# A new order for the first 560 steps of an attention and MLP kernel, without five of its eight identity products

## The chip, the cores and the metric

The kernel runs on one core of one Trainium2 chip. The metric is device time in microseconds (us). The kernel before takes 633.52 us, the median of three runs (633.43 to 633.88). The profile used below is one further execution of it.

## The reference

```python
def _attn_ref(q, k, v):                       # (4, 8, 768, 64) each
    k_sum = k.reshape(B, H, nb, 32, D).max(axis=3)
    v_sum = v.reshape(B, H, nb, 32, D).mean(axis=3)
    scores_l = scale * np.matmul(q, k.transpose(0, 1, 3, 2))
    mask_l = np.abs(pos[:, None] - pos[None, :]) < 16
    scores_s = scale * np.einsum('bhsd,bhnd->bhsn', q, k_sum) + np.log(32)
    scores_all = np.concatenate([np.where(mask_l, scores_l, -1e9), scores_s], axis=-1)
    a = softmax(scores_all)
    return np.matmul(a, np.concatenate([v, v_sum], axis=2))
def _moe_ref(x, w_in, w_out):                 # x (3072, 512), d_ff 2048
    h = x @ w_in
    return ((h * np.cos(h)) @ w_out).astype(np.float32)
```

Each query sees the keys nearer than 16 positions and 24 block summaries. The attention output, heads side by side, is the x of the MLP.

## The kernel before, in words

The 3072 tokens are eight blocks of 384 (0 to 7). Two blocks make one batch entry. In a block the eight heads are four pairs, called a, b, c, d: `a0` is the first pair of block 0. The MLP of a block runs over 16 slices of d_ff; slice `w5` is 128 columns of w_in and 128 rows of w_out. One slice applied to one block is a step, `s0` to `s127`; s0 to s5 are block 0 with slices 0 to 5, s6 to s21 are block 1, s22 to s31 the rest of block 0.

Nothing is scheduled by the compiler. The string `ORDER` lists some 2,100 tokens. Each token calls one method, and the tokens' order is the order in which each engine's queue receives its instructions. An engine takes its own in that order and waits at the first that is not ready. The semaphores between engines follow from which tile or PSUM bank an instruction reads and writes. A token has a name, a step and arguments: numbers are PSUM banks or buffers, and a letter at the end is the engine (a = ScalarE, v = VectorE, p = GpSimd). All loads and stores sit in SyncE's queue, but for the very last store.

The tokens that matter here, in the order in which a pair goes through them, for blocks 0 and 1:

- `q`, `k` load the pair (L454); `tq`, `tk` transpose it on TensorE (L503, L516); `cq`, `ck` copy the result out of PSUM (L509 or L511, L370 or L372), and `ks` takes the block maxima of k (L535, VectorE).
- `ms` puts the masks into two PSUM banks (L554), `sc` adds the scores (L579), `mx` takes the row maxima (L597, VectorE, two instructions), `ex` the exponentials (L614, ScalarE, six instructions), `iv` the inverse of the sums (L624 and L627), `nm` multiplies by it (L630, GpSimd).
- `tp` transposes the probabilities (L639), `cp` copies them out (L370 or L372), `v` loads the value windows (L475, L483), `m` copies the value summaries beside them, `va` is the product with the values (L683). `xh` and `xl` split the result into two parts, the MLP's input (L370 or L372, L376).
- The means of v come from `vm` and `ve` for batch entry 0, and for entry 1 from loads `v1_0.l`, `v1_1.l`, ... (L246), each followed by its sum `v1_0.s`, ... (L261 on VectorE, L251 and L270 on GpSimd). These loads share one buffer: `v1_1.l` waits until `v1_0.s` is done, `v1_2.l` until `v1_1.s` is done.
- A weight slice is loaded by `l` (L391, L395) as packed bytes, and unpacked by `ab` and `sh` (ScalarE, L403, L409), `fb` (VectorE, L416), `hi` (L370 or L372) and `lo` (L376).
- A step is `u` in four chunks, one for each pair's x, or `up` in one piece (L738, L726); `tu`, `re`, `si`, `ga` are the gate (L746, L749, L754, L758); `hi` and `lo` split it; `dh` and `dl` are the products with w_out (L786).

The eight `h` tokens are products of the identity with itself (L930, 128x512) whose result nothing reads:

```python
        def products(self, i):
            nc.tensor.matmul(
                out=bank(i), lhsT=ident, rhs=ident.unsqueeze(1).broadcast_to([P, DM // P, P]), start=True, stop=True
            )
```

Three of them (h0, h2, h4) come before the first transposes, five (h7, h5, h1, h6, h3) between the attention's products of the first 30 us.

Of the kernel before, what the change touches and what calls it, by code (L numbers as in the profile page):

```python
# [47 lines left out]
s5.lo.1.v w9.hi.a w6.l.6 s6.tu.1 s10.up.6 w8.lo.p a2.v a2.m s3.re s6.re s5.dh s3.si s3.ga s3.hi.1.v w7.ab.1 w9.lo.v
s4.dl s3.lo.0.p s4.dh s3.dh v1_5.s.v w7.sh w10.ab.0 s3.dl s5.dl w7.fb w7.hi.v s6.si s6.ga s8.up.2 s6.hi.0.v w10.sh
s11.tu.0 s6.lo.0.v w10.fb s5.ta.0.a s10.tu.1 w10.hi.a w10.lo.p w7.lo.v s9.up.4 s11.re s10.re s5.ta.1.v s11.si s10.si  # L50
w6.ab.1 s7.up.1 s11.ga v1_6.l s10.ga w12.l.7 v1_6.s.v s10.hi.1.a w6.sh s10.lo.1.v v1_7.l s6.dh.5.7.6 w6.fb w12.ab.0
s11.hi.0.a s6.dl s11.lo.0.v w6.hi.a s5.ta.2.v s7.tu.1 s8.tu.0 s7.re s10.dh s11.dh s10.dl v1_7.s.v s11.dl w12.sh s7.si
s8.re w13.l.6 s7.ga s16.up.0 s8.si s8.ga s8.hi.1.a s15.up.1 w12.fb s7.hi.0.a s14.up.2 a2.k s5.st.0 w6.lo.v w12.hi.a
w13.ab.1 s7.lo.1.p s7.dh a2.kt.1 s15.tu.1 s5.st.1 s15.re w13.sh s5.st.2 s8.lo.0.p w12.lo.v s15.si s15.ga w15.l.7
a2.kt.0 b2.k s8.dl s8.dh w13.fb w11.l.6 s14.tu.0 s15.hi.0.a s14.re s14.si s7.dl s15.lo.0.v s16.tu.1 s15.dh s15.dl
s16.re s14.ga s14.hi.1.v s14.lo.1.p s12.up.3 w13.hi.a a2.ks.1 s16.si s16.ga a2.q s16.hi.0.a s16.lo.0.v s12.tu.0
b2.kt.0 w15.ab.0 s13.up.1 w13.lo.v w15.sh s18.up.0 s19.up.2 b2.kt.1 s13.tu.1 a2.ks.0 c2.k w15.fb b2.ks.0 w11.ab.1
w11.sh b2.ks.1 s12.re s16.dl s14.dh s12.si s13.re w11.fb s16.dh s12.ga w15.hi.a a2.qt s12.hi.1.a s14.dl w11.hi.v
s13.si s12.lo.0.v c2.kt.0 s13.ga s18.tu.0 s13.hi.0.a w14.l.6 w11.lo.p s18.re s18.si s18.ga s12.dh s18.hi.1.v s12.dl
s13.lo.1.v s19.tu.1 c2.kt.1 s18.lo.0.p s19.re d2.k s9.tu.0 s13.dh s9.re w14.ab.1 s19.si w15.lo.p s9.si w14.sh s18.dh  # L60
s18.dl s13.dl s19.ga s9.ga w14.fb s19.hi.0.a w14.hi.a a2.kw.v s9.hi.1.v s17.up.0 s23.up.3 b2.q a2.sc.2.1 w14.lo.p
b2.kw.a s19.lo.0.v d2.kt.1 d2.kt.0 a2.z.1 s19.dh a2.z.0 s19.dl a2.mx.2 s17.tu.1 s17.re s17.si s9.dh b2.qt s17.ga c2.q
# [974 lines left out]
```

## Time and profile before

| | |
|---|---|
| median of three runs | 633.52 us |
| profiled execution, its own time | 633.6 us |
| its span, first to last instruction | 631.9 us |
| TensorE busy | 621.1 us, 98% |
| VectorE, ScalarE, GpSimd busy | 422.1, 323.9, 204.6 us |

The span is what the profile shows; 1.7 us of the execution's own time lie outside it. Matmul ends are modelled: a TensorE instruction may look busy until the next one starts. In a timeline row the first number is the start and the second the time from there to the end of the row's last instruction.

### The profile page before, as it was taken

To read this page: it belongs to the slowest core of one execution; us is meant where nothing else is said; L and a number is where in the kernel's file an instruction comes from. 1 tells how busy PE (TensorE), PEld (TensorE's weight loads), DVE (VectorE), ACT (ScalarE), POOL (GpSimd) and SP (SyncE) were. 2 spreads that over 40 slices of the span, in tenths; PEclk is the share of its full clock that TensorE was granted. 3 is DMA by queue.
4 is the path that set the end of the run, shared out by engine and by line. 5 is a ranking of instruction groups with operands and counts; after the bars stand their busy time and mean duration, and the time that the engine had idled before them with its cause. 6 is when DMAs were issued, how large, how long until landed. Compare 5 with 4: busy or idle time off the path is not lost.

```text
span 631.9 us, 12130 instructions
## 1 busy us (share of the span) xinstructions
PE 621.1 (98%) x4568; PEld 544.3 (86%) x4568; DVE 422.1 (67%) x814; ACT 323.9 (51%) x606; POOL 204.6 (32%) x218
## 2 busy tenths in 40 slices
PE   8989999999999999999999999999999999999997
...
PEclk9999999999999999999999999999999999999999
...
GB/s 223 261 220 272 297 123 250 145 54 123 122 143 133 112 95 174 102 61 108 109 110 126 117 93 102 121 47 77 108 98 61 117 75 56 114 35 17 1 1 50
DMA packets 170058, 73.52 MB, mean 116 GB/s; under 512 B 136848, under 2 KB 158864, under 8 KB 170000
## 3 DMA queue, kind: packets, MB, share of 16 engines
...
q14 instruction: 22, 0.18, 0.1%
...
## 4 chain that ended last, share of the span: by engine, by line
PE 92%; DVE 4%; SPq 2%; DMA 1%; issue 1%; ACT 1%; POOL 0%; POOLq 0%; DVEq 0%
PE banks L786 41%; PE banks L726 40%; PE banks L683 3%; PE banks L567 3%; PE banks L930 1%; SPq L475 1%; DVE stage L416 1%; PE banks L738 1%; PE banks L579 1%; SPq L483 1%; PE banks L516 0%; PE banks L909 0%; DMA late<-in_v_dram 0%; DMA x<-in_v_dram 0%; DVE kd L535 0%
## 5 line engine op out<-in xcount | busy, mean ns | idle before, releaser
L726 PE MATMUL banks<-xh,w 128*128 128x384 f32 x976 | 255.5, 337 | 0.5 <-DVE t L758 0.5
L786 PE MATMUL banks<-w,gh 128*128 128x512 f32 x768 | 196.5, 392 | 0.1
L726 PEld LDWEIGHTS banks<-xh,w 128*128 128x128 f32 x976 | 176.8, 188 | 3.1 <-issue 0.8
L786 PEld LDWEIGHTS banks<-w,gh 128*128 128x128 f32 x768 | 142.6, 188 | 31.4 <-DVE gh L372 1.8
L726 PE MATMUL banks<-xl,w 128*128 128x384 f32 x488 | 163.2, 334 | 0.0
L376 POOL TENSOR_TENSOR gl<-t,gh 128x384 fp32r<-128x384 f32 x63 | 65.9, 1048 | 283.3 <-DVE gh L372 147.8
L746 ACT ACTIVATE t<-banks 128x384 int32<-128x384 f32 x128 | 62.0, 488 | 126.8 <-PE banks L726 59.7
L749 DVE SCALAR_TENSOR_TENSOR t<-t,banks 128x384 f32<-128x384 int32 x128 | 69.1, 546 | 68.3 <-ACT t L746 67.6
L786 PE MATMUL banks<-w,gl 128*128 128x512 f32 x384 | 108.0, 392 | 0.0
L754 ACT ACTIVATE t<-t 128x384 f32<-128x384 f32 x128 | 65.9, 523 | 63.4 <-DVE t L749 63.1
L726 PEld LDWEIGHTS banks<-xl,w 128*128 128x128 f32 x488 | 91.6, 188 | 0.4
L758 DVE TENSOR_TENSOR t<-t,banks 128x384 f32<-128x384 f32 x128 | 69.4, 547 | 33.1 <-ACT t L754 32.1
L786 PEld LDWEIGHTS banks<-w,gl 128*128 128x128 f32 x384 | 71.6, 188 | 15.7 <-POOL gl L376 0.5
L370 ACT CAST gh<-t 128x384 fp32r<-128x384 f32 x66 | 33.5, 511 | 43.5 <-DVE t L758 25.5
L630 POOL TENSOR_TENSOR sc<-sc,r 128x720 f32<-128x720 f32 x28 | 39.0, 1392 | 43.5 <-DVE r L627 41.0
L602 POOL TENSOR_TENSOR sc<-sc,m 128x720 f32<-128x720 f32 x24 | 34.3, 1433 | 49.6 <-DVE m L594 49.6
L376 DVE TENSOR_TENSOR gl<-t,gh 128x384 fp32r<-128x384 f32 x65 | 36.8, 569 | 12.5 <-ACT gh L370 7.5
L372 DVE CAST gh<-t 128x384 fp32r<-128x384 f32 x62 | 23.1, 373 | 18.1 <-PE banks L786 14.9
L586 DVE SCALAR_TENSOR_TENSOR sc<-banks,mask 128x360 f32<-128x360 f32 x48 | 24.5, 523 | 12.5 <-PE banks L567 12.2
L620 DVE TENSOR_REDUCE r<-sc 128x6 f32<-128x726 f32 x24 | 21.6, 902 | 13.8 <-ACT sc L609 13.8
L376 POOL TENSOR_TENSOR w<-stage,w 128x1024 fp32r<-128x1024 f32 x8 | 19.8, 2470 | 31.3 <-DVE w L372 20.0
L609 ACT ACTIVATE sc<-sc 128x720 f32<-128x720 f32 x24 | 19.4, 807 | 19.0 <-POOL sc L602 18.8
...
## 6 DMA issues: line engine op xcount, KB each, us to landing
...
```

The lines of the kernel that those rows point to most:

```text
L370: eng.copy(out=out, in_=in_)
L372: eng.tensor_copy(out=out, in_=in_)
L376: eng.tensor_tensor(out=lo, in0=src, in1=hi.bitcast(F32), op=ALU.subtract)
L586: nc.vector.scalar_tensor_tensor(out=self.sc.rearrange("p (c h) n -> p c h n", h=2)[:, :, hh, :], in0=self.sp[hh], scalar=SCALE, in1=mask[ ...
L602: nc.gpsimd.tensor_tensor(out=self.sc, in0=self.sc, in1=self.m.unsqueeze(2).broadcast_to([P, U, NK]), op=ALU.subtract)
L630: nc.gpsimd.tensor_tensor(out=self.sc, in0=self.sc, in1=self.r.unsqueeze(2).broadcast_to([P, U, NK]), op=ALU.mult)
L726: nc.tensor.matmul(out=self.h, lhsT=w_of(name, self.f)[:, c * P : (c + 1) * P], rhs=x_of(self.blk, part, c), start=n == 0, stop=n == last,)
L746: nc.scalar.activation(out=self.t.bitcast(I32), in_=self.h, func=AF.Copy, scale=1.0 / TWO_PI, bias=0.25)
L749: nc.vector.scalar_tensor_tensor(out=self.t, in0=self.t.bitcast(I32), scalar=-TWO_PI, in1=self.h, op0=ALU.mult, op1=ALU.add)
L754: nc.scalar.activation(out=self.t, in_=self.t, func=AF.Sin, scale=-1.0, bias=-0.5 * math.pi)
L758: nc.vector.tensor_tensor(out=self.t, in0=self.t, in1=self.h, op=ALU.mult)
L786: nc.tensor.matmul(out=accs[self.run][i], lhsT=g[:, i * P : (i + 1) * P], rhs=w_of(name, self.f), start=self.first and n == 0, stop=self.l ...
```

## The change

`ORDER` alone is changed. It has 2,093 tokens instead of 2,098: h7, h5, h1, h6 and h3 are gone, h0, h2 and h4 stay. Every other token is there once, as before. SyncE's queue (loads and stores) keeps its order exactly. On TensorE, VectorE, ScalarE and GpSimd the order is new up to `c2.z.0` in block 2, and from there to the end the two strings are the same but for line breaks. In the new part 58 tokens change between VectorE, ScalarE and GpSimd, and many take other PSUM banks. Cut to the part up to the first product with w_out:

```diff
-h0.w.3 h2.w.0 h4.w.1 a0.k a0.q b0.q a0.tk.1.5 c0.k a0.tk.0.0 a0.ms.7.6 a0.ks.1 d0.k b0.tq.3 a0.ks.0 b0.k a0.tq.4 c0.q
-a0.ck.1.a a0.ck.0.a h7.w.5 b0.cq.a a0.cq.v a0.sc c0.tk.0.0 c0.tk.1.2 b0.tk.0.4 c0.ks.0 c0.ck.0.a a0.mx.0 w1.l.6 h5.w.1
-a1.q c0.tq.0 h1.w.1 d0.q a0.ex.0 c0.ck.1.v b0.ck.0.a d0.tk.0.6 c0.ks.1 a0.iv b0.tk.1.1 b0.ks.0 d0.tk.1.2 c0.ms.3.7
-c0.cq.v b0.ms.5.0 c0.sc v0_0.l d0.ck.1.a d0.ks.1 b0.ck.1.a d0.ks.0 b0.ks.1 d0.ck.0.v b0.sc w1.ab.0 b1.q w1.sh c0.mx.1
-h6.w.2 a1.tq.6 a1.ms.1.4 v0_1.l v1_0.l d0.tq.2 a1.cq.v c0.ex.1 d0.cq.a a1.sc d0.ms.6.2 d0.sc b0.mx.2 c1.q w1.fb a0.nm
-w1.hi.v a0.tp.1.3 b0.ex.2 v0_0.vm.0 d0.mx.0 d0.ex.3 v0_1.vm a0.v a0.cp.1.a w1.lo.p c0.iv a1.mx.1 v0_1.ve.a b0.iv
-b1.tq.5 a0.tp.0.3 b1.cq.v b1.ms.2.6 b1.sc w0.l.7 d0.iv c0.nm b0.nm a0.m.p d0.m.p b0.m.p d1.q v1_0.s.0.v a1.ex.0 h3.w.5
-a0.cp.0.v d1.m.p b1.mx.2 c0.m.p c1.tq.3 v1_1.l c0.tp.0.5 d0.nm c0.v a1.iv a1.nm a1.m.p c0.tp.1.0 a0.va.4 c1.ms.7.1 c1.cq.v
-c0.cp.0.v d1.tq.3 d0.v a0.xh.a c1.sc v1_1.s.p w2.l.6 b0.v d1.cq.v a0.xl w0.ab.1 b0.tp.1.3 b0.tp.0.5 c0.cp.1.v w0.sh
-d0.tp.0.4 c0.va.0 b1.ex.1 d0.tp.1.6 v1_2.l c1.mx.0 w5.l.1 w0.fb w0.hi.v a1.v w0.lo.p d0.cp.0.a c1.ex.2 b1.iv d0.cp.1.v
-c1.m.p d1.ms.4.2 c0.xh.v d1.sc c0.xl d0.va.0 b1.nm d1.mx.1 b0.cp.0.a b0.cp.1.v a1.tp.0.7 w2.ab.1 c1.iv a1.tp.1.6 c1.nm
-s1.u.0.3 w2.sh d0.xh.v d1.ex.3 d0.xl b0.va.1 b0.xh.v s0.u.0.5 b0.xl v1_2.s.p s0.u.2 s1.u.2 s1.u.3 a1.cp.0.v c1.tp.1.7
-s1.u.1 s0.u.3 w2.fb w2.hi.v a1.cp.1.a d1.iv d1.v c1.v c1.tp.0.2 s0.u.1 s1.tu.0 w4.l.6 w5.ab.0 a1.va.4 s0.tu.1 w2.lo.v
-w5.sh v1_3.l s0.re d1.nm s1.re s2.u.0.6 s2.u.2 s2.u.3 c1.cp.0.a d1.tp.1.1 c1.cp.1.v c1.va.2 d1.tp.0.0 w3.l.7 s0.si
-w5.fb w5.hi.v d1.cp.1.a b1.tp.0.7 w5.lo.v s1.si s1.ga s0.ga d1.cp.0.a b1.v s2.u.1 d1.va.1 b1.tp.1.0 s5.u.0.5 a1.xh.a
-c1.xh.a w8.l.0 a1.xl s1.hi.0.a s0.hi.1.a d1.xh.v d1.xl s1.lo.0.v s0.lo.1.v w4.ab.1 b1.cp.1.a w4.sh v1_3.s.v s5.u.2
-s2.tu.0 s5.u.3 s2.re b1.m.p v1_4.l s5.u.1 w4.fb s0.dh.1.0.3 s2.si s0.dl s2.ga s2.hi.1.v s2.lo.1.p w3.ab.0 b1.cp.0.v
...
+h0.w.3 h2.w.0 h4.w.1 a0.k a0.q a0.tk.1.2 b0.q c0.k a0.ks.1 a0.tk.0.7 a0.ck.0.a d0.k a0.tq.1 a0.ck.1.a a0.cq.a b0.k
+a0.ks.0 c0.tk.1.6 a0.ms.7.0 c0.q w1.l.6 a0.sc a0.mx.0 c0.tk.0.1 c0.ms.2.3 c0.ck.0.v a0.ex.0 d0.tk.0.7 c0.ks.0 c0.ck.1.v
+b0.tk.0.5 a1.q b0.tq.0 d0.tk.1.4 a0.iv b0.ck.0.v a0.nm d0.q d0.ks.0 b0.tk.1.1 d0.ck.0.a d0.ck.1.v v0_0.l b1.q c0.tq.7
+v0_1.l b0.cq.a v1_0.l d0.ks.1 c0.ks.1 a0.tp.0.0 b0.ks.0 c1.q a0.cp.0.v c0.cq.a a0.v w1.ab.1 w0.l.7 c0.sc v1_0.s.0.p
+a1.tq.0 d0.tq.6 b0.ms.7.5 d1.q c0.mx.1 v1_1.l c0.ex.1 b0.ks.1 a1.cq.v b0.ck.1.v c0.v b0.sc w1.sh d0.cq.v b0.mx.2
+b0.ex.2 w1.fb d0.v w2.l.6 d0.ms.3.4 w1.hi.a a1.ms.2.1 d0.sc a1.sc d0.mx.0 a0.tp.1.7 v0_0.vm.6 a0.cp.1.v c0.iv a1.mx.1
+b1.tq.0 b0.iv d0.ex.3 v0_1.vm v0_1.ve.a b1.cq.v d0.iv c0.nm d0.nm b0.m.p b0.v c1.tq.5 a1.m.p c1.ms.0.6 c1.cq.v a1.ex.0
+c0.tp.1.2 b0.nm c0.m.p v1_1.s.p v1_2.l w5.l.1 w1.lo.v a1.v d0.m.v c1.sc a1.iv c1.mx.2 c0.tp.0.7 a0.m.a b1.ms.1.4
+a0.va.3 d1.v a0.xh.v w0.ab.0 c1.ex.2 b1.sc c0.cp.0.a a1.nm c1.v d1.tq.0 c0.cp.1.v d0.tp.0.2 w0.sh a0.xl b0.tp.1.6
+b1.mx.0 c0.va.3 d0.tp.1.5 b0.tp.0.7 c1.iv d1.cq.v c0.xh.a d0.cp.0.v c0.xl d0.cp.1.a d0.va.5 w0.fb b0.cp.1.v s1.u.0.3
+b1.ex.1 d0.xh.a d1.ms.1.2 d1.sc a1.tp.0.0 w0.hi.v w0.lo.v w2.ab.1 c1.nm s0.u.0.6 d1.mx.0 s0.u.2 s1.u.2 d0.xl w2.sh
+b0.cp.0.a w2.fb w4.l.6 b0.va.7 b0.xh.v d1.ex.3 w2.hi.v b0.xl s0.u.3 s1.u.3 c1.tp.1.5 a1.tp.1.1 d1.iv a1.cp.0.a s0.u.1
+a1.cp.1.v w2.lo.v s1.u.1 w5.ab.0 v1_2.s.p a1.va.0 w5.sh b1.iv s0.tu.0 c1.cp.1.v c1.tp.0.7 s2.u.0.2 a1.xh.a s2.u.2
+c1.m.p w5.fb c1.cp.0.a d1.nm a1.xl w5.hi.a s2.u.3 s2.u.1 s0.re s1.tu.1 s0.si v1_3.l c1.va.4 d1.tp.1.5 d1.tp.0.7 w5.lo.v
+s1.re d1.m.p d1.cp.1.a s1.si d1.cp.0.v s0.ga s5.u.0.0 s5.u.2 s1.ga w3.l.7 c1.xh.a s5.u.3 s0.hi.1.a s0.lo.0.v b1.nm
+w4.ab.1 s1.hi.0.v s1.lo.1.p c1.xl d1.va.7 s2.tu.0 s2.re b1.tp.0.1 w4.sh b1.v b1.tp.1.3 s2.si s5.u.1 s5.tu.1 b1.cp.0.a
+w4.fb s0.dh.5.6.4 s2.ga s2.hi.1.v s5.re s0.dl s1.dh s1.dl w4.hi.a s2.dh s5.si w4.lo.v s4.u.0.2 d1.xh.a d1.xl s4.u.2
...
```

## Rows read from the trace of the kernel before

**Rows 1.** The page: TensorE in 40 equal slices, and its granted clock, in tenths.
```profile
PE   8989999999999999999999999999999999999997
...
PEclk9999999999999999999999999999999999999999
```

**Rows 2.** Busy time of each engine by stretch, then granted clock, DMA share, GB/s.
```profile
35.00:40.00 5.00, 3.32 (x87) 2.43 (x87) 4.90 (x9) 4.37 (x25) 4.63 (x7) 1.00 0.92 253
40.00:50.00 10.00, 8.71 (x108) 7.48 (x103) 8.93 (x16) 8.25 (x20) 9.62 (x8) 1.00 0.89 209
```

**Rows 3.** Timeline of TensorE: identity products (L930) and what follows the last.
```profile
1.44 5.49 PE L930 MATMUL banks<-ident 128*128 128x512 f32 x6 [1.44 <-POOL ident masks.py:199]
...
28.87 1.12 PE L930 MATMUL banks<-ident 128*128 128x512 f32 x2
29.83 0.49 PE L503 MATMUL banks<-ident,late 128*128 128x128 f32 x3
```

**Rows 4.** Timeline of TensorE: d1.tq, c1.sc, a1.va (49.19), s5.u.0, s0.dh (58.30).
```profile
32.53 0.52 PE L503 MATMUL banks<-ident,qn 128*128 128x128 f32 x3 [0.29 <-DMA qn<-in_q_dram]
32.98 1.09 PE L579 MATMUL banks<-kd,qd 64*64 64x96 f32 x48
...
49.19 0.91 PE L683 MATMUL banks<-pt,late 120*64 120x64 f32 x22 [0.27 <-DMA late<-in_v_dram]
...
56.10 0.44 PE L738 MATMUL banks<-xh,w 128*128 128x384 f32 x1 [0.41 <-DVE t L758]
...
58.30 1.55 PE L786 MATMUL banks<-w,gh 128*128 128x512 f32 x6
```

**Rows 5.** Timeline of SyncE's queue: loads v1_0, d1.q (26.10), v1_1 and v1_2.
```profile
19.63 1.07 SPq L246 DMA_DIRECT2D kn<-in_v_dram  x1
...
26.10 0.91 SPq L454 DMA_DIRECT2D qn<-in_q_dram  x2
29.05 0.34 SPq L246 DMA_DIRECT2D kn<-in_v_dram  x1
...
39.97 0.32 SPq L246 DMA_DIRECT2D kn<-in_v_dram  x1
```

**Rows 6.** Timeline of GpSimd: c0.nm, one m copy, and the four operations of v1_1.s.
```profile
26.20 1.39 POOL L630 TENSOR_TENSOR late<-late,r 128x720 f32<-128x720 f32 x1
...
31.31 0.83 POOL L372 COPY late<-early 24x768 f32<-24x768 f32 x1
...
37.57 1.59 POOL L251 TENSOR_TENSOR kn<-kn 96x256 f32<-96x256 f32 x2
39.24 0.71 POOL L270 TENSOR_TENSOR vs<-vs,kn 96x64 f32<-96x64 f32 x2
```

**Rows 7.** Groups by form, 8 to 62 us: operation xcount | busy, mean ns | idle before.
```profile
L597 DVE TENSOR_REDUCE m<-banks 128x3 f32<-128x360 f32 x16 | 7.7, 523 | 0.0
...
L376 DVE TENSOR_TENSOR xl<-banks,xh 128x384 fp32r<-128x384 f32 x6 | 3.3, 554 | 0.1
L376 DVE TENSOR_TENSOR w<-stage,w 128x1024 fp32r<-128x1024 f32 x2 | 2.4, 1205 | 0.0
...
L614 ACT ACTIVATE sc<-banks,m 128x120 f32<-128x120 f32 x24 | 8.3, 368 | 0.0
...
L403 ACT ACTIVATE stage<-late 128x1024 f32<-128x1024 int8 x6 | 6.9, 1148 | 1.0 <-POOL w L376 1.0
L409 ACT ACTIVATE first<-stage 128x1024 int8<-128x1024 f32 x5 | 6.9, 1374 | 0.1
```

**Rows 8.** Timeline of VectorE: unpacking of slices w0, w2 and w4.
```profile
35.23 1.58 DVE L416 SCALAR_TENSOR_TENSOR stage<-late,first 128x1024 int32<-128x1024 int32 x1
36.84 1.20 DVE L372 CAST w<-stage 128x1024 fp32r<-128x1024 f32 x1
...
44.97 2.09 DVE L416 SCALAR_TENSOR_TENSOR stage<-late,first 128x1024 int32<-128x1024 int32 x1 [0.33 <-POOL sc L630]
...
60.44 1.21 DVE L416 SCALAR_TENSOR_TENSOR stage<-late,first 128x1024 int32<-128x1024 int32 x1
```

More of the change, by code (lines that the diff above doesn't have):

```diff
@@ L48 @@
[L48 to L62, printed above, removed]
@@ new lines @@
+v1_3.s.v s4.u.3 b1.m.p b1.cp.1.a w3.ab.0 s2.lo.1.p w8.l.0 w3.sh v1_4.l s4.u.1 s2.dl s5.ga b1.va.7 s5.hi.1.a b1.xh.a
+w9.l.1 w3.fb s5.dh s4.tu.0 b1.xl s11.up.3 s4.re w8.ab.1 s4.si w7.l.7 w3.hi.v s4.ga w3.lo.v w8.sh s6.up.2 w8.fb
+s4.hi.0.a v1_4.s.0.p s5.lo.0.v s3.u.0.1 w9.ab.0 s3.u.2 v1_5.l s3.u.3 w9.sh w10.l.2 w8.hi.v s3.u.1 s4.lo.1.v s3.tu.1
+w9.fb s3.re s6.tu.0 s4.dl w8.lo.p s3.si s6.re s10.up.7 w9.hi.a s3.ga s3.hi.1.a s3.lo.1.p s6.si v1_5.s.v s6.ga s4.dh
+s3.dh w9.lo.v s3.dl w6.l.6 w7.ab.1 s10.tu.1 s6.hi.1.v w7.sh s10.re s5.dl s10.si s15.up.1 s5.ta.0.a w7.fb s10.ga w7.hi.a
@@ new lines @@
+s10.hi.0.v a2.v s6.lo.1.p s10.lo.0.v s8.up.2 s5.ta.1.v s11.tu.0 s6.dh.5.7.6 s11.re w10.ab.0 s11.si s6.dl w7.lo.p a2.m
+w10.sh s11.ga s5.ta.2.v v1_6.l s11.hi.1.a s7.up.4 w10.fb s11.lo.1.v w6.ab.1 w6.sh v1_6.s.v s8.tu.1 s10.dh s11.dh
+w10.hi.a w12.l.7 w6.fb v1_7.l s7.tu.0 w10.lo.v s8.re s7.re w6.hi.a s7.si s7.ga w13.l.6 s10.dl w12.ab.0 s14.up.3
+v1_7.s.v s11.dl s8.si a2.k s7.hi.0.a s7.lo.0.v s8.ga s16.up.0 w12.sh w6.lo.p s15.tu.0 s5.st.0 s8.hi.1.a s5.st.1
+s13.up.2 s7.dh s15.re w12.fb s15.si s15.ga s8.lo.1.v s12.up.4 w13.ab.1 s8.dl a2.kt.0 s8.dh s7.dl s16.tu.1 s15.hi.0.v
@@ new lines @@
+s30.si b3.kw.a b3.qt s30.ga c2.xh.a s30.hi.0.a a3.z.0 s31.re s31.si s31.ga s28.dl s29.dh s29.dl s31.hi.1.a s31.lo.0.v
+s30.lo.1.p s30.dh s30.dl s31.dh s31.dl v2_4.s.1.v a3.z.1 a3.mx.0 c2.xl a3.su b3.sc.2.1 d2.pi d2.va.0 d2.xh.v d2.xl
+s32.up.6 s32.tu.1 s32.re s32.si s32.ga s32.hi.0.a v2_5.l v2_5.s.p s31.fe.1.0 s31.ad.1 s33.up.0 s36.up.7 s34.up.4
+s33.tu.0 s33.re b3.z.0 s32.lo.1.v s33.si s33.ga s33.hi.1.v a3.ex.0 s34.tu.1 s31.fe.2.1 s31.ad.2 s38.up.0 b3.z.1 b3.mx.1
+v2_6.l s31.st.1 s34.re a3.sm c3.kw.a s35.up.1 s34.si s34.ga s32.dh.2.4.5 s34.hi.0.a s32.dl s33.dh s33.lo.0.p s33.dl
@@ new lines @@
+s54.re s56.up.3 b4.iv s53.si s53.ga s51.dh c4.mx.0 b4.nm c4.su s51.dl s52.dh s53.hi.0.a s53.lo.1.v s55.tu.0 s54.si
+s55.re s54.ga s54.hi.1.a s52.dl s54.lo.0.p s53.dh s53.dl s54.dh s54.dl s55.si s56.tu.1 b4.pt.1 s55.ga s55.hi.0.v b4.po
+s56.re s56.si c4.ex.2 v3_2.s.p v3_3.l a4.va.0 a4.xh.v d4.sc.2.6 s56.ga d4.z.0 d4.z.1 s59.up.7 s57.up.6 s60.up.2
+s58.up.3 a5.qt c4.sm s56.hi.1.v s56.lo.1.p s57.tu.1 s57.re d4.mx.1 a5.kw.a s55.lo.0.p s59.tu.0 c4.iv s59.re c4.nm
+s59.si v3_3.s.v s57.si s57.ga s55.dh s55.dl s56.dh s57.hi.0.a s57.lo.0.v a4.xl s58.tu.1 s56.dl s57.dh s57.dl a5.sc.0.6
```

202 lines of the change are left out of this document (98 added, 104 removed).

## The prediction

> **What bounds the kernel now.** I read the page's slices first. From the third slice of 15.8 us to the last, TensorE is at nine tenths or more and its clock is full [rows 1]. What is done there is the same before and after, so the change can gain only in the first 60 us, and it gains what TensorE no longer spends there on waits or on work that nothing reads. The stretches come next: from 35 to 40 us TensorE is busy 3.32 us of 5, VectorE 4.90, GpSimd 4.63; from 40 to 50 GpSimd is busy 9.62 of 10 and VectorE 8.93 [rows 2]. There the other engines feed TensorE, not the reverse. Last I read the timelines for who waits. TensorE waits at d1.tq for a load, at a1.va for a load, and at 56.10 for a gate on VectorE; the first product with w_out (s0.dh) starts at 58.30 [rows 4]. Both orders put the same TensorE work ahead of s0.dh, the five products apart. So I follow the new order to s0.dh, and the difference there is the gain, if nothing waits later.
>
> **The five products.** The last holds TensorE from 28.87 to 29.83, 0.96 us [rows 3]; five are 4.8 us. They are worth 4.8 us if TensorE is never short of work in their place, and nothing if it waits there. So the rest of the sum is about waits.
>
> **The loads.** SyncE's order is unchanged, but its waits are not. The new order gives v1_0.s to GpSimd and puts it ahead of c0.nm. v1_0.l is issued from 19.63 to 20.70 [rows 5]. No row shows its landing: not before 20.70, and not after about 28, since its sum on VectorE was done when v1_1.l went out at 29.05. The nearest row is d1.q: issued by 27.01, and the transposes waited for it until 32.53, so 5.5 us [rows 4, 5]. v1_0 is one transfer where d1.q is two, so I take 5.2 us: 25.9. On GpSimd the two halvings take 1.67 us (37.57 to 39.24) and one addition half of 0.71 [rows 6]: done at 27.9. v1_1.l can go at 28.0 instead of 29.05, and the loads behind it move up by 1.05 us. v1_1.s stands on GpSimd behind what the next part adds up to 34.5, takes 1.67 + 0.71 [rows 6] and ends at 36.9; v1_2.l, which waits for it, went at 39.97 [rows 5], so there the loads gain up to 3 us. a1.v, which stopped TensorE at 49.19, then lands near 47 and does not bind below.
>
> **GpSimd and TensorE, 26 to 36 us.** c0.nm ran at 26.20 [rows 6]; now it stands behind v1_0.s, from 27.9 to 29.3. Behind it on GpSimd are d0.nm, b0.m, a1.m, b0.nm and c0.m: two nm of 1.37 and three copies of 0.83, done at 34.5. On TensorE c0.tp.1 waits for c0.nm, and behind it c1.sc, c0.tp.0, b1.ms, a0.va, b1.sc, d1.tq, d0.tp.0, b0.tp.1 and c0.va are queued. c1.sc (1.05 us start to end of use [rows 4]) is over at 30.7. Until c0.va come c0.tp.0 0.45, b1.ms 0.4, a0.va 0.9 as a1.va's row, b1.sc 1.05, d1.tq 0.45 (three transposes, 32.53 to 32.98 [rows 4]), d0.tp.0 0.5 and b0.tp.1 0.3 (four and two of them): 4.1 us. So c0.va runs from 34.8 to 35.7. d1.q has landed by 32.5 and binds no more. This stretch spends the gain: five products are gone, and the wait for c0.nm and the block behind it stand in their place.
>
> **ScalarE and VectorE, 31 to 48 us.** c1.mx takes 0.96 us (7.7 over 8 pairs), c1.ex 2.1 (8.3 over 4) [rows 7], then c0.cp and w0.sh (1.37) end near 35.7, beside c0.va. c0.xh and c0.xl, 0.55 each, follow c0.va: VectorE gets to w0.fb at 36.8, where it was at 35.23 before [rows 8]. From here VectorE works without a gap, in the new order: w0.fb 1.58, b0.cp.1 0.35, w0.hi 1.13, w0.lo 1.2 (it was GpSimd's, and costs VectorE the mean of rows 7) to 41.1; d1.mx 0.96, d0.xl 0.55, w2.fb 2.09, b0.xh 0.55, w2.hi 1.1, b0.xl 0.5 to 46.8. w2.fb costs 2.09 by its own row and 1.21 by w4.fb's [rows 8]; GpSimd was busy beside the first and idle beside the second, and v1_2.s will be on GpSimd then, so I take 2.09. w0.fb likewise keeps its 1.58. With 1.21 for both the chain is 1.25 us shorter. w2.ab before waited 1.0 us for a buffer that w0.lo held on GpSimd [rows 7]; it now has another buffer and waits only for its load, and w2.sh ends at 42.1, ahead of VectorE. Then s0.u.1, which needs b0.xl, and s1.u.1, 1.3 us with their first weight load, and a1.va starts at 48.1 and ends at 49.0, where it ended at 50.10 (49.19 and 0.91 [rows 4]). That is 1.1 us.
>
> **From there to s0.dh.** The new order has c1.tp.0 (0.4 us) still to do, which the old one had done. The old one still waited 0.41 at 56.10. These cancel. From a1.va's start TensorE has a1.va 0.9, c1.tp.0 0.4, four chunks of s2 2.2 (as s5's, 56.10 to 58.30 [rows 4]), c1.va 0.9 and d1.tp 0.8: s5.u.0 at 53.3. It needs w5.lo, and VectorE has from b0.xl to there w2.lo and w5.lo at 1.2, w5.fb at 1.6 to 2.1, a1.xl and s0.re at 0.55, and four small ones of 0.3: 6.3 to 6.8 us, so 53.1 to 53.6. That is next late, by nothing or by 0.3 us. Behind it are four chunks 2.2, d1.va 0.9 and b1.tp 0.8: s0.dh at 57.2 instead of 58.30. Later the order and engines of some 150 us change, and every TensorE slice there is full [rows 1]; I count nothing, because the same producers stand about as far ahead of their users, and a move between VectorE and GpSimd is covered by TensorE's own work. If that cover failed, each late lo part would cost up to its own 1.2 us.
>
> Sum, on the profiled execution's 633.6 us (span 631.9 and 1.7 outside; its median is 633.52): 633.6 - 1.1 = **632.5 us**. From both sides: TensorE alone allows -4.8, the chain with both fb at their cheapest -2.4, and with v1_0 landing at 28 instead of 25.9 the same chain is 2.1 later, +1.0.
>
> **The rivals.** First, the products' time comes back in larger part: VectorE's unpacking is cheap, and c0.nm is early because v1_0 lands well before 25.9. For it: w4.fb's 1.21 [rows 8]. Against: GpSimd's 9.62 of 10 [rows 2]. The first alone gives -2.4, 631.2 us; without any wait it ends at -4.8, 628.8.
>
> Second, a wash: v1_0 lands late or VectorE's list slips, and GpSimd's blocked queue pays back all of the 1.1 us. From a landing at 27.0 on, the change gives nothing: 633.6 us. For it: c0.nm is 1.7 us later, by a wait the old order did not have. Against: d1.q's 5.5 us is already among the slow ones. In this sense the change would not do what its dropped work says.
>
> Third, the clock, on the slower side. The first three products ran in 5.49 us, 1.83 each, where the last took 0.96 [rows 3]: TensorE starts at 1.2 GHz and later works at 2.4. The five products fill its thin stretches between 9 and 30 us. Without them it is thinner still from 11 to 16 us: d0.tk and b0.tq go into banks that a0.ex reads for 2.1 us, and a0.tp waits for a0.nm's 1.39 [rows 6, 7]. If the clock falls there and is still low at 29.3, c0.tp.1 to c0.va, 5.5 us of TensorE's own work on the chain, runs at 1.9 times its time. From 1.2 us of such work on, the 1.1 us are gone; 3.5 us of it cost 3.1: 635.6 us. Against it: from 35 to 40 us TensorE worked 3.32 of 5 us with no identity product, and the clock stayed at 1.00 [rows 2].
>
> The Trainium skill, "TensorE: Matmul & The Clock Gate", section "A second HAM failure mode: psum-queue depth-cycling", says that a TensorE with many short idle times between groups of matmuls swings between the two clocks. By that rule the third rival happens, 635.6 us; by the row of 35 to 40 us it does not, and the forecast stands. The trace leans against the rule, but its thin stretch is shorter and denser than the new one.
>
> **How the numbers follow.** Forecast 632.5 (own range 631.4 to 633.2): 0.46. More of the products' time back (628.8 to 631.4): 0.21. Wash (633.2 to 634.8): 0.15. Clock (634.8 to 638): 0.18. What can be told from no change is 0.2%, 1.27 us, so faster means under 632.25. Of the forecast's 0.46 some 0.2 lie there: faster 0.41; within 0.2% the other 0.26 and the wash, 0.41; slower 0.18. The range goes from 629.8 to 635.6, which leaves out half of the clock case and the far end of the first rival.
>
> **What would show it.** Right: no identity product after 7 us and granted clock 1.00 throughout; v1_0.s on GpSimd ending near 28 and c0.nm near 29.3; TensorE waiting there; w0.fb near 36.8, later than before; v1_2.l near 37; s0.dh near 57.2; no new wait of TensorE after 60 us. Wrong: c0.nm at 26 or before, a1.va still waiting for its load, a TensorE clock of 0.5 after 8 us, or waits past 60 us.

## The result: slower by 1%

The changed kernel takes 640.17 us (median of 4 runs, 639.06 to 641.55) against 633.51 (633.43 to 633.88) for the kernel before on the same chip: a ratio of 1.0105, 95% interval 1.0082 to 1.0128. The forecast was 632.5, and the range ended at 635.6. The profiled execution is the fastest of the four, 639.06 us with a span of 637.3, so the trace lags by 5.4 us; what made the others slower than it stands in no trace. TensorE's lag at the start of equal work was 1.13 us at s0.dh (59.43 against 58.30) and 5.40 us at d2.sc (164.38 against 158.98), and it stayed there; between the two both orders have the same TensorE work. So 1.1 us were lost in the front, up to s0.dh, and 4.3 us in the tail, from s0.dh to d2.sc, for which the prediction counted nothing. In the rows of after, kernel lines are numbered one lower than before, as `ORDER` is a line shorter.

**The page after.** First busy time by engine, then the slices of TensorE and its clock [rows 1]:

```profile
PE 620.0 (97%) x4558; PEld 542.9 (85%) x4558; DVE 431.7 (68%) x813; ACT 325.8 (51%) x607; POOL 203.7 (32%) x222
...
PE   6989989999999999999999999999999999999997
...
PEclk9989999999999999999999999999999999999999
```

TensorE's sixth slice (80 to 96 us) is no longer at nine tenths, and the clock has one gap. VectorE is busy 9.6 us longer than before (422.1).

**The stretches** [rows 2], and two of the tail:

```profile
35.00:40.00 5.00, 4.76 (x102) 3.79 (x106) 4.05 (x5) 4.51 (x17) 4.69 (x7) 1.00 1.04 236
40.00:50.00 10.00, 8.10 (x72) 6.52 (x67) 8.72 (x15) 7.91 (x18) 4.29 (x7) 0.83 0.91 194
80.00:90.00 10.00, 8.90 (x44) 7.39 (x42) 9.63 (x12) 8.15 (x12) 5.77 (x3) 1.00 0.85 248
90.00:100.00 10.00, 8.34 (x40) 7.15 (x41) 8.71 (x14) 7.76 (x11) 1.43 (x1) 1.00 0.24 70
```

From 40 to 50 us TensorE is busy less than before and its clock is 0.83 on average. From 80 to 100 us TensorE is no longer full, and VectorE is at 9.63 of 10.

**w0.fb** [rows 8] on VectorE's timeline, and GpSimd's beside it:

```profile
37.60 3.55 DVE L415 SCALAR_TENSOR_TENSOR stage<-late,first 128x1024 int32<-128x1024 int32 x1
41.08 0.41 DVE L371 COPY pt<-banks 120x256 f32<-120x256 f32 x1
41.41 0.68 DVE L371 CAST w<-stage 128x1024 fp32r<-128x1024 f32 x1
42.12 1.23 DVE L375 TENSOR_TENSOR w<-stage,w 128x1024 fp32r<-128x1024 f32 x1
```
```profile
37.34 1.39 POOL L629 TENSOR_TENSOR sc<-sc,r 128x720 f32<-128x720 f32 x1
38.68 1.39 POOL L629 TENSOR_TENSOR late<-late,r 128x720 f32<-128x720 f32 x1
```

The unpacking took 3.55 us. It is issued at 37.60, while GpSimd has a1.nm running; c1.nm follows at once, and the unpacking ends at 41.15, 1.1 us after GpSimd's end at 40.07. GpSimd's two ran in their clean 1.39 us each. So VectorE's operation stood until 40.07, rather than running slower. Behind it TensorE waited for w0.hi and w0.lo and came to s0.dh late [rows 4]:

```profile
42.14 0.44 PE L737 MATMUL banks<-xh,w 128*128 128x384 f32 x1 [1.26 <-DVE w L371]
42.42 0.34 PE L737 MATMUL banks<-xl,w 128*128 128x384 f32 x1
43.40 1.01 PE L737 MATMUL banks<-xh,w 128*128 128x384 f32 x2 [0.64 <-DVE w L375]
...
59.43 1.55 PE L785 MATMUL banks<-w,gh 128*128 128x512 f32 x6
```

**The tail** has three waits of TensorE of 0.8 us or more (s3.dh, s6.dh, s7.up) and one of 0.2 at 152.19, where before had none from 58 to 175 us:

```profile
81.64 1.66 PE L785 MATMUL banks<-w,gh 128*128 128x512 f32 x6 [0.88 <-ACT gh L369]
...
90.88 0.73 PE L785 MATMUL banks<-w,gh 128*128 128x512 f32 x2 [1.10 <-DVE late L371]
...
93.08 0.44 PE L725 MATMUL banks<-xh,w 128*128 128x384 f32 x1 [0.79 <-DVE late L371]
```

The four add up to 3.0 us, and the lag grew by 4.3. The other 1.3 us stand in no row as a wait (a TensorE instruction may look busy until the next one starts), so how they split is open. The first goes back to w9.fb, which stood behind w8.lo (75.53 to 78.13 on GpSimd). VectorE's row, then GpSimd's with w8.lo and w7.lo:

```profile
76.14 3.08 DVE L415 SCALAR_TENSOR_TENSOR stage<-late,first 128x1024 int32<-128x1024 int32 x1 [0.27 <-ACT first L408]
```
```profile
75.53 2.60 POOL L375 TENSOR_TENSOR w<-stage,w 128x1024 fp32r<-128x1024 f32 x1 [1.15 <-DVE w L371]
...
87.40 2.41 POOL L375 TENSOR_TENSOR w<-stage,w 128x1024 fp32r<-128x1024 f32 x1 [0.28 <-ACT w L369]
```

The second and third are s5.ta.1 and s5.ta.2 (they free TensorE's banks), queued on VectorE behind s10.lo, 2.78 us from 87.44 where it took 0.55 before, beside w7.lo on GpSimd.

**The chain that ended last** says it in one view (start, length, what). Before, from 62.64 us, it is TensorE alone; after, it goes mostly through VectorE and ScalarE, and comes back to TensorE for good only at 152.19:

```profile
76.44 6.16 PE banks L786 x27
82.61 6.26 PE banks L726 x36
88.87 6.35 PE banks L786 x27
```
```profile
76.14 3.08 DVE stage L415
79.22 0.48 DVE t L748
79.72 0.53 ACT t L753
80.27 0.56 DVE t L757
80.83 0.96 DVE part_sum L260
...
87.44 2.78 DVE gl L375
90.22 0.60 DVE late L371
...
152.19 3.06 PE banks L785 x12
```

### The profile page after: what moved, and what is told of

It is laid out like the page before. It is cut to its first block, busy times and chain, and to the rows that moved or that the text cites. A ratio compares the mean times of both kernels' runs of the same rounds, so it can differ in the third digit from the quotient of the medians.

```text
span 637.3 us, 12131 instructions
## 1 busy us (share of the span) xinstructions
PE 620.0 (97%) x4558; PEld 542.9 (85%) x4558; DVE 431.7 (68%) x813; ACT 325.8 (51%) x607; POOL 203.7 (32%) x222
## 4 chain that ended last, share of the span: by engine, by line
PE 79%; DVE 9%; ACT 4%; DMA 2%; issue 2%; SPq 2%; POOL 0%; DVEq 0%; ACTq 0%; POOLq 0%
PE banks L785 36%; PE banks L725 34%; PE banks L682 4%; PE banks L566 3%; DVE stage L415 2%; SPq L453 2%; DVE w L375 1%; ACT first L408 1%; PE banks L737 1%; ACT stage L402 1%; DVE gl L375 1%; DMA qn<-in_q_dram 1%; DVE t L748 1%; DMA kn<-in_k_dram 1%; DMA late<-in_moe_w_out_dram 1%
## 5 line engine op out<-in xcount | busy, mean ns | idle before, releaser
L375 POOL TENSOR_TENSOR gl<-t,gh 128x384 fp32r<-128x384 f32 x66 | 69.5, 1054 | 290.3 <-DVE gh L371 137.5
L375 DVE TENSOR_TENSOR gl<-t,gh 128x384 fp32r<-128x384 f32 x62 | 38.4, 621 | 11.6 <-ACT gh L369 6.6
L652 DVE STREAM_TRANSPOSE stage<-sc 128x768 f32<-128x768 f32 x24 | 23.3, 973 | 7.3 <-POOL sc L629 7.2
```

The costliest lines, as they stand in the source:

```text
L375: eng.tensor_tensor(out=lo, in0=src, in1=hi.bitcast(F32), op=ALU.subtract)
```

## The experiments

Front is the order through s0.dh, tail the rest up to where the two orders agree. Theory A: VectorE's operations stand behind GpSimd's, and TensorE then waits for VectorE's queue. B: TensorE's clock falls for want of the identity products. C: the loads of v and w come late. D, from the fourth set on: only the order in which things become ready counts, not the meeting of the two engines. All times stand beside the kernel before on the same chip, which took 633.6 to 633.8 us.

**e1: only the products go.**
```diff
- ... h7.w.5 ... h5.w.1 ... h1.w.1 ... h6.w.2 ... h3.w.5 ...
```


> The order of before, with only its last five identity products left out. Theory A (the loss is the new order: VectorE and GpSimd hold each other up, and TensorE waits where it did not before): the products go without a loss, at most 4.8 us are gained, and what TensorE waits in their place takes most of it; 631 to 633.6 us. Theory B (the loss is the products: without them TensorE's clock falls in the thin stretch): a granted clock of 0.5 appears after 8 us and the time goes up by 2 us or more, to 635.5 or above.


632.94 us (632.47 to 633.85), ratio 0.9986 (0.9977 to 0.9996). s0.dh comes at 57.21, 1.09 us earlier, and the tail has no wait; at d2.sc 0.75 us of it are left (158.23 against 158.98), and the median is 0.7 lower. So 0.7 us of the products' 4.8 reach the end; nearly all of the rest is waited for. B as written falls.

**e2: new front, old tail.**
```diff
- ... b1.cp.0.a w4.fb s0.dh.5.6.4 s2.ga s2.hi.1.v s5.re s0.dl s1.dh s1.dl w4.hi.a s2.dh ...
+ ... v1_4.l s0.dh.1.5.3 s0.dl s2.ga s2.hi.1.v s2.lo.0.p w3.ab.0 w4.hi.a s1.dh s1.dl s2.dh ...
```


> The new order up to the first product with w_out (s0.dh, 59.4 us in the profile of after, 58.3 before), then all that is left in the order and on the engines of before, and no identity products. Theory A: the front alone costs its 1.1 us and the old tail has no new wait: 634 to 635.5 us. Theory B (the clock): the same front holds the fall to 0.5 near 43 us, so 1.1 us are all that it costs; the two theories differ in the cause, not in this time. Theory C (the loads come late because of the new front, and the waits at 80 to 95 us follow from it): the tail's loss stays, 638 us or more.


639.58 us, ratio 1.0093 (1.0075 to 1.0110). It lies in C's range, but it tells nothing of the front: TensorE waited 2.7 us at s0.dh for ScalarE to read a bank that b1.tp still held (the old tail's bank for s0.dh), and its granted clock was 0.66 from 60 to 65 us. e12 repeats it without that bank.

**e3: old front, new tail.**
```diff
- ... s0.dh.1.0.3 s2.si s0.dl s2.ga s2.hi.1.v s2.lo.1.p w3.ab.0 b1.cp.0.v c1.xl ...
+ ... s0.dh.3.4.1 s2.ga s2.hi.1.v s5.re s0.dl s1.dh s1.dl w4.hi.a s2.dh s5.si ...
```


> The order of before with its identity products up to s0.dh, then the rest in the order and on the engines of after. Theory A: the tail brings its own losses, some 4.3 us (the lag of after behind before grows from 1.1 us at s0.dh to 5.4 at 160 us): 636.5 to 638.5 us, with TensorE's waits at s3.dh, s6.dh and s7.up again. Theory B (clock, products): nothing of the loss is left, 633 to 634 us. Theory C (loads late through the front): about as before, 633 to 634.5.


642.65 us, ratio 1.0147 (1.0130 to 1.0164). The lag is 0.2 us at s0.dh and 6.2 at d2.sc. 19 operations of the tail have other banks than in after, so that no bank is taken while in use. So the tail loses by itself, more than A's 4.3 and outside A's 636.5 to 638.5. Its waits are not at s3.dh, s6.dh and s7.up as A had them (the longest are 1.4 us at 102.74 and 1.0 at 122.88), and what the other banks have in it wasn't separated. B and C, which had the loss come from the front, fall for the tail.

**e4: two products into the idle time ahead of s0.u.0.**
```diff
- ... c1.nm s0.u.0.6 ...
+ ... c1.nm h7.w.4 h5.w.4 s0.u.0.6 ...
```


> The new order as it is, and two identity products put on TensorE just ahead of s0.u.0, where it was idle for 1.3 us in the profile of after before its clock fell at 43.0 us. Theory A: the waits for w0.hi and w0.lo stand, the products hide in them, and the time stays near 640 (639 to 641), whether the clock falls or not; a full clock from 43 to 46.4 us gives back at most 1.5 us of TensorE's work there, of which some is waited for anyway. Theory B: the clock stays at 1.00 through 50 us and the time goes down by 1.5 us or more, to 638.5 or less.


639.69 us, ratio 1.0099 (1.0084 to 1.0115): within the spread of after. The clock held:
```profile
40.00:50.00 10.00, 9.45 (x125) 7.29 (x122) 9.93 (x15) 8.74 (x20) 5.25 (x7) 1.00 1.01 206
```
s0.dh came 0.6 us earlier than in after, and the tail took that back. The clock's fall at 43 us is not the loss, and B falls.

**e5: five operations moved in the tail.**
```diff
- ... w9.fb s3.re ... w9.hi.a s3.ga s3.hi.1.a ... s10.lo.0.v s8.up.2 s5.ta.1.v ... s5.ta.2.v ...
+ ... s3.re ... s3.ga w9.fb s3.hi.1.a w9.hi.a ... s5.ta.1.v s5.ta.2.v s10.lo.0.v s8.up.2 ...
```


> The new order with five operations moved inside the tail: on VectorE w9.fb goes behind s3.ga (on ScalarE w9.hi behind s3.hi), and s5.ta.1 and s5.ta.2 go ahead of s10.lo. No load, no engine and nothing ahead of 70 us changes. Theory A (VectorE's long SBUF operations stand behind GpSimd's, and what is queued behind them makes TensorE wait): the waits at s3.dh, s6.dh and s7.up (0.9, 1.1 and 0.8 us) go, and the time falls by 2 to 3.5 us, to 636.5 to 638. Theory C (the loads come some 7 us late, and the waits follow from that): w9's parts are no earlier, and the time stays at 639 to 641.


637.94 us (636.43 to 638.73), ratio 1.0065 (1.0048 to 1.0081), 2.2 us less than after. w9.fb took 1.22 us, the waits at s6.dh and s7.up are gone, and one of 1.6 us for a gate on VectorE came in their place. A's range holds, C's doesn't, and the moved queue is late somewhere else.

**e6: w0.fb earlier.**
```diff
- ... d0.cp.0.v c0.xl d0.cp.1.a d0.va.5 w0.fb ...
+ ... w0.fb d0.cp.0.v c0.xl d0.cp.1.a d0.va.5 ...
```


> The new order with w0.fb moved on VectorE ahead of d0.cp.0 and c0.xl, so that it starts near 36.3 us, while GpSimd has no normalization running. Theory A: w0.fb takes 1.2 to 2 us instead of 3.55, w0.hi and w0.lo are 1.5 to 2.5 us earlier, TensorE's wait at s0.u.0 mostly goes, and s0.dh comes near 57.5 to 58.5 instead of 59.4; the time falls by 1 to 2 us if the tail doesn't change, to 638 to 639. Theory B (the clock): whether it falls depends on the idle time at 41 to 43 us, which goes here too, so the same sign. Theory C: no change, 639 to 641.


640.17 us, ratio 1.0103 (1.0088 to 1.0118). w0.fb took 1.34 us and s0.dh came at 57.80, 1.6 us earlier than in after. The time did not move, so A's 638 to 639 was missed: TensorE waited 2.6 us for gates in the tail where it had waited 0.9. The tail is set by VectorE and ScalarE, so TensorE coming earlier only waits longer.

**e7: e5 and e6 together.**
```diff
- ... d0.cp.0.v c0.xl ... w0.fb ... w9.fb s3.re ... s10.lo.0.v s8.up.2 s5.ta.1.v ...
+ ... w0.fb d0.cp.0.v c0.xl ... s3.re ... s3.ga w9.fb ... s5.ta.1.v s5.ta.2.v s10.lo.0.v s8.up.2 ...
```


> Both edits together: w0.fb ahead of d0.cp.0 and c0.xl, and the five operations moved in the tail. Theory A: the two gains add, as they lie in different stretches: 634.5 to 637 us. Theory C: 639 to 641.


637.26 us (636.82 to 639.84), ratio 1.0065 (1.0045 to 1.0086). s0.dh is 1.4 us earlier than in before, and d2.sc 2.8 later. The gains don't add, for e6's reason, and A's 634.5 to 637 was too low.

**e8: v1_3's sum, and with it the loads, earlier.**
```diff
- ... s0.lo.0.v b1.nm ... d1.xl v1_3.s.v s4.u.3 ...
+ ... s0.lo.0.v v1_3.s.v b1.nm ... d1.xl s4.u.3 ...
```


> The new order with only v1_3.s moved up on VectorE, to right behind s0.lo (where the order of before has it), so that v1_4.l, and w9.l, w7.l and v1_5.l behind it on SyncE, go out 5 to 6 us earlier, near 60 to 62 us instead of 66 to 68. Theory C (late loads are the cause): the waits at s3.dh, s6.dh and s7.up go and the time falls by 2.5 us or more, to 637.5 or less. Theory A: the loads move up, VectorE's queue around s2.re and w4.fb is 1.65 us later instead, and the time changes by less than 1 us either way: 639 to 641.


642.10 us (639.30 to 642.60), ratio 1.0118 (1.0095 to 1.0142). v1_4.l went out at 61.27 instead of 66.30, and the waits of 1.1 and 0.8 us at s6.dh and s7.up stayed; s3.dh's fell from 0.9 to 0.5. C falls: its 637.5 was not reached by any execution. A's 639 to 641 was missed too. The profiled execution, the slowest, came to s0.dh 1.5 us later than after, with its clock low for longer near 45 us, and there was a second fall right behind those waits:
```profile
95.00:100.00 5.00, 4.98 (x18) 4.76 (x19) 4.92 (x6) 4.97 (x8) 0.00 (x0) 0.67 0.12 41
```

**e9 and e10: order and engines apart.** e9 has the new order, with the 30 operations of the tail that changed engine put back; e10 has the old order without the products, and those 30 as after has them.
```diff
- e9: ... w8.hi.v ... w7.lo.p ... w10.lo.v ... w15.lo.v ...
+ e9: ... w8.hi.a ... w7.lo.v ... w10.lo.p ... w15.lo.p ...
- e10: ... w8.hi.a ... w10.lo.p w7.lo.v ... w15.lo.p ...
+ e10: ... w8.hi.v ... w10.lo.v w7.lo.p ... w15.lo.v ...
```


> The new order as it is; behind s0.dh the 30 operations that changed their engine go back to the engine of before. By now theory A is: in the tail (60 to 150 us) the chain of waits runs through VectorE and ScalarE, because VectorE's SBUF operations stand behind GpSimd's (11.1 us of stretch there against 2.8 before). It has two forms. A1, the engine moves make the stretch: the stretch falls under 5 us and the time to 634 to 637 us. A2, the order makes it (which of the two engines' operations meet, and how late the producers start): the time stays at 638 to 642.

> The order of before without its last five identity products; behind s0.dh the 30 operations go to the engine that they have in after. A1 (the engine moves): the loss comes without the new order, 635 us or more. A2 (the order): near the 632.9 us of the order of before without the products, 632.4 to 634.


640.59 us, ratio 1.0113 (1.0098 to 1.0128), and 640.88, ratio 1.0115 (1.0100 to 1.0130). A1 and A2 both fall as alternatives: either half alone brings a loss as large as after's. In e10 the place is seen. VectorE and GpSimd, then TensorE's waits from 58 to 175 us:
```profile
83.83 2.02 DVE L416 SCALAR_TENSOR_TENSOR stage<-late,first 128x1024 int32<-128x1024 int32 x1 [0.24 <-ACT first L409]
86.97 2.23 DVE L376 TENSOR_TENSOR w<-stage,w 128x1024 fp32r<-128x1024 f32 x1 [1.12 <-ACT w L370]
```
```profile
83.76 1.01 POOL L376 TENSOR_TENSOR gl<-t,gh 128x384 fp32r<-128x384 f32 x1 [4.82 <-DVE gh L372]
84.73 3.38 POOL L376 TENSOR_TENSOR w<-stage,w 128x1024 fp32r<-128x1024 f32 x1
```
```profile
PE banks L786 <- DVE t L758: 3.0, 1, 3.0
PE banks L567 <- DVE qd L521: 1.4, 1, 1.4
PE banks L786 <- POOL gl L376: 0.6, 1, 0.6
```
w10.fb (1.22 in e1) stands 0.8 us and w10.lo 1.0 beside GpSimd; TensorE waits 3.0 us for the gate queued behind them.

**e11 and e12: new front, old tail, with TensorE's banks renamed through s0.dl so that e2's wait can't come; e11 also has e6's edit.**
```diff
- ... s0.dh.5.6.4 s2.ga s2.hi.1.v s5.re s0.dl s1.dh s1.dl w4.hi.a s2.dh ...
+ ... s0.dh.1.0.3 s2.ga s2.hi.1.v s5.re s0.dl w8.l.0 d1.xh.v d1.xl b1.cp.1.a v1_3.s.v ...
```


> The new front (through s0.dl) with w0.fb ahead of d0.cp.0 and c0.xl, TensorE's banks renamed so that the old tail fits behind it, then the order and the engines of before. Theory A: s0.dh 0.5 to 1.4 us earlier than before and no wait behind it: 632.2 to 633.4 us, perhaps ahead of both kernels. If the new front hands too little over to the tail (its producers late), waits come behind s0.dh all the same: 635 us or more.

> The same with the new front as it is: the first hybrid again, now without the bank of s0.dh that another product still held. Theory A: 1.1 us late at s0.dh and constant from there, 634 to 635.5 us, so the new front costs 1 us and the new tail the other 5. If the front hands too little over: 637 us or more.


e12: 635.76 us (635.18 to 636.37), ratio 1.0031 (1.0018 to 1.0044), 0.3 above A's range. e11: 634.46, ratio 1.0012 (0.9993 to 1.0030), between its two forecasts. So by medians the new front costs 2.8 us against e1, about half of it w0.fb's. In e12's trace 1.9 us stand at s0.dh (59.09 against 57.21), and the old tail behind it has two waits of 0.3 us. e11's ten runs lie apart by the clock: eight with a mean granted clock of 0.996 or more took 633.21 to 635.30, two with 0.992 took 638.45 and 638.82. The profiled one is of those two. There c0.tp.1 to c0.va, the stretch that the third rival named, ran at the lower clock; it fell behind a wait of 2.53 us for c0.nm and not in 11 to 16 us:
```profile
30.00:35.00 5.00, 4.91 (x72) 3.87 (x74) 1.78 (x5) 3.13 (x13) 4.79 (x6) 0.50 1.23 239
```

**e13 and e14: spare work on GpSimd.** The order of e1, with seven bursts of six products of a tile with itself, which nothing reads.
```diff
+            for _ in range(6):
+                nc.gpsimd.tensor_tensor(out=ident, in0=ident, in1=ident, op=ALU.mult)
```


> The order of before without its last five identity products, and on GpSimd seven bursts of six multiplications of a dead 128x128 tile with itself, put in between 63 and 96 us where GpSimd had nothing to do (one each behind s2.lo and w3.lo, two behind s3.lo, three behind w10.lo). Nothing waits for them. Theory A (GpSimd's operations hold up VectorE's, and VectorE is nearly full there): VectorE's operations stretch by 5 us or more in sum, TensorE gets waits between 65 and 120 us, and the time goes up by 2 to 8 us from 632.9, to 635 to 641. Theory D (what costs is only the order in which things are ready, not the two engines' meeting): no change, 632.5 to 633.5.

> The same seven bursts, put in between 258 and 290 us (behind s45.lo, s46.lo, s47.lo twice and s50.lo three times), where VectorE has more idle time. Theory A: VectorE's operations stretch as much, but the stretch finds idle time and TensorE waits less: 632.5 to 634. If blocking costs the same everywhere: 635 to 641, as the run before. Theory D: 632.5 to 633.5.


638.01 us, ratio 1.0063 (1.0049 to 1.0078), and 637.95, ratio 1.0062 (1.0049 to 1.0075). Both cost 5 us. D's 632.5 to 633.5 was missed in both and A's 632.5 to 634 in e14, but neither tells the theories apart: a burst took 3.1 us (three in 9.30) to 4.9 us beside VectorE, and GpSimd's own work behind it came late (TensorE waited 1.6 us for one low part on GpSimd in e13, 1.1 in e14). In e14 VectorE's busy time rose by only 0.6 us, so there it is GpSimd's queue; in e13 it rose by 3.9, and both have a part. A's claim that the place matters was not shown.

**e15: two low parts exchanged in e1.**
```diff
- ... w10.lo.p w7.lo.v ...
+ ... w10.lo.v w7.lo.p ...
```


> The order of before without its last five identity products, with two low parts exchanged between the engines as after has them: w7.lo to GpSimd, w10.lo to VectorE. Theory A: w7.lo's 2.4 us on GpSimd stand beside w10.fb and w10.lo on VectorE, which stretch to about 2 us each, s8's gate is late and TensorE waits near 88 us: 3 to 5 us more than 632.9, 635.5 to 638. Theory D: an exchange of equal work, 632.5 to 633.7.


636.46 us (635.87 to 638.22), ratio 1.0045 (1.0030 to 1.0060), 3.5 us above e1. s6.hi, 0.36 us in e1, stands behind w7.lo. e1's row of it, then e15's of VectorE, GpSimd and TensorE:
```profile
82.05 0.36 DVE L372 CAST gh<-t 128x384 fp32r<-128x384 f32 x1
```
```profile
82.95 0.55 DVE L758 TENSOR_TENSOR t<-t,banks 128x384 f32<-128x384 f32 x1
83.60 2.12 DVE L372 CAST gh<-t 128x384 fp32r<-128x384 f32 x1
85.86 0.56 DVE L376 TENSOR_TENSOR gl<-t,gh 128x384 fp32r<-128x384 f32 x1
```
```profile
83.12 2.40 POOL L376 TENSOR_TENSOR w<-stage,w 128x1024 fp32r<-128x1024 f32 x1 [2.40 <-DVE w L372]
```
```profile
91.94 1.20 PE L786 MATMUL banks<-w,gh 128*128 128x512 f32 x4 [2.13 <-DVE t L758]
```
That is 1.76 us. w10.lo on VectorE then stands at the head of the queue for w10.hi, 1.1 us. VectorE's lag behind e1 grows by 2.96, from 1.56 to 4.52 us, and TensorE waits 2.13. Its clock then falls:
```profile
90.00:95.00 5.00, 3.06 (x10) 2.43 (x11) 4.79 (x9) 4.60 (x6) 0.00 (x0) 0.84 0.08 30
95.00:100.00 5.00, 5.00 (x20) 4.08 (x20) 4.55 (x9) 4.42 (x8) 0.00 (x0) 0.82 0.68 214
```
16% and 18% of 5 us below full speed are 1.7 us of TensorE's work, so wait and clock give 3.8 in this execution. It is the slowest of the four, 638.22, and 1.5 of its 5.3 us over e1's were there at s0.dh, ahead of the exchange. The execution whose mean clock was 1.0 took 635.87, so without the fall the exchange still costs 2.9. A holds, and D falls as the only cause: 1.76 us are the two engines' meeting, the 1.1 behind w10.hi are a matter of the order. That w10.fb and w10.lo would be the ones that stand was wrong, s6.hi was.

**e16: b0.v's load earlier in e1.**
```diff
- ... v1_1.l ... w2.l.6 b0.v ...
+ ... b0.v v1_1.l ... w2.l.6 ...
```


> The order of before without its last five identity products, with b0.v moved up on SyncE to right ahead of v1_1.l, where SyncE waits 2.0 us for v1_0's sum. b0.va is what TensorE waited for 1.5 us at 42.2 us. If that load sets the end of the front: 0.5 to 1.5 us less, 631.4 to 632.4. If VectorE's queue is next late: no change, 632.4 to 633.4. If the loads behind it (c0.v, d0.v) now come late: 633.5 or more.


633.48 us (632.46 to 635.21), ratio 0.9995 (0.9985 to 1.0005): no gain on e1. The wait for b0.v went, and s0.dh came at 57.20. In both runs TensorE waits 0.5 us at 55.02 for a gate on VectorE, so that is next late. In e16's chain that gate goes back, over ScalarE, to GpSimd's queue from 42.1 to 50.5 us, so VectorE's queue is only the last part of it.

## Why the prediction was wrong

By medians the loss splits in this way: 633.6 before, -0.7 for the products (e1), +2.8 for the new front (e12 against e1), +4.4 for the new tail (after against e12): 640.1. The split is that of this sequence: behind the old front the new tail costs 9.0 (e3, with 19 other banks).

**The products, right.** 4.8 us alone, and waits in place of most of it. e1 gives back 1.1 at s0.dh and 0.7 at the end.

**The loads and GpSimd's block, right.** v1_0's sum on GpSimd ended at 27.2 us (27.9 predicted), c0.nm ran to 28.69 (29.3), and TensorE waited 0.94 at c0.tp.1, as forecast. The row names another releaser beside c0.nm, the exponentials of a1 on ScalarE, which had to leave the bank and did so at about the same time (28.7 to 28.8):

```profile
28.95 0.41 PE L638 MATMUL banks<-ident,late 128*120 128x128 f32 x2 [0.94 <-ACT sc L613]
```

v1_1.l went at 27.22 (28.0), v1_2.l at 37.40 (37). c0.va began at 35.49 (34.8).

**w0.fb, the step of the front that failed.** "w0.fb likewise keeps its 1.58" [rows 8]: it took 3.55, from 37.60 (36.8 predicted). The row's 1.58 was no property of the operation, it was how much of it stood behind one GpSimd operation then. In the new order one normalization ran beside it and a second came behind. s0.dh came at 59.43 instead of 57.2. With w0.fb at 1.34 (e6) it came at 57.80, so some 1.6 of the 2.2 us are w0.fb's, what the clock lost behind its wait included (e4, with the clock held, gave 0.6 at s0.dh). Other prices of the same list erred the other way, and that was luck: w2.fb, taken at 2.09, was 1.36, and w0.hi and w2.hi, taken at 1.13 and 1.1, were 0.68 each.

The Trainium skill, "SBUF — State Buffer", section "Who interferes with whom", says that where a VectorE operation and one of GpSimd contend for their shared port, the one that issues first holds it for its whole instruction, and the other blocks. The trace agrees for w9.fb and s10.lo in after and s6.hi in e15 (3.08, 2.78 and 2.12 us beside GpSimd; 1.22, 0.55 and 0.36 without). For w0.fb's 3.55 it goes beyond that: the second normalization started at 38.68, after w0.fb's 37.60, and still went first.

**"I count nothing" after 60 us, the step that cost most.** It rested on two reasons. "The same producers stand about as far ahead of their users" read TensorE's full slices [rows 1] as slack, but they don't say how far ahead the producers are. "A move between VectorE and GpSimd is covered by TensorE's own work" priced a failed cover at the 1.2 us of one low part. In its place the runs show that TensorE's full slices in the old tail hang on its own pairing of order and engines: a new order with the old engines (e9), the old order with new engines (e10) and one exchange of two operations (e15) lose 6.8, 7.9 and 3.5 us against before, e1 and e1 (e9 has the new front's loss in it). Over stretches of 20 us VectorE is busy 8.5 to 9.2 of 10 us from 60 to 120 us in both kernels, which leaves little idle time to make up what stands there. In e15 a block of 1.76 us led to 3.5 us by median, through the head of VectorE's queue and TensorE's wait, and in some executions the clock. How the 4.4 us split over the single meetings wasn't separated; e5 shows 2.2 of them at w9.fb and s10.lo, and the cause of the other half is argued from the same rows, not shown.

**The clock rival, on the right side and at another place.** In after the granted clock was 1.00 from 10 to 20 us and 0.50 from 43.0 to 46.4, behind waits of 1.26 and 0.64 us. Held at full (e4) it gains 0.5 us, within the spread. Where the rival put the fall it came in one execution without the products, that of e15, whose front is e1's:

```profile
15.00:20.00 5.00, 5.00 (x109) 4.02 (x108) 3.80 (x8) 3.61 (x7) 1.39 (x1) 0.67 1.19 283
```

At 42 us TensorE was no later for it than in e1 (b0.va at 42.06 against 42.36, both behind its load); whether the 1.5 us at s0.dh come from it is not shown. In the tail of e10 and e15 the fall is a second price beside the wait. The prediction also read the first three products' 1.83 us as a clock of 1.2 GHz; the granted clock of that stretch is 1.00 in the profile, so that reading is not shown. No rival put the loss behind 60 us, so the range could not hold it.

**Best version.** e1, 632.94 us, is ahead of both kernels, of before by 0.1%; nothing tried on it gained more.
